# 64-bit weights to float32 with one joining in place of two, and new due times, in an attention and two-layer kernel

## The chip, the cores and the metric

The kernel runs on one core of a Trainium2 chip. The metric is the device time of one execution in microseconds (us); lower is better. The engines are called TensorE (PE in the rows, its weight loads PEld), VectorE (DVE), ScalarE (ACT), GpSimd (POOL) and SyncE (SP, which issues nearly all DMAs).

## What is computed

Random-feature attention over 4 batches, 8 heads, 576 tokens, head size 64 and 128 features, then two dense layers on the 2304 x 512 result, each with 2048 hidden units. The attention inputs and the result are float32, the dense weights come as float64.

```python
def phi(x):
    proj = np.einsum('bhsd,md->bhsm', x, omega)
    h = proj - np.sum(x * x, axis=-1, keepdims=True) / 2.0
    return np.exp(h - np.max(h, axis=-1, keepdims=True)) / np.sqrt(m)
num = phi(q) @ (phi(k).T @ v);  den = phi(q) @ phi(k).sum(tokens) + 1e-06
x = num / den                              # 2304 x 512
x = softplus(x @ w_in) @ w_out             # layer 0
out = silu(x @ w_in2) @ w_out2             # layer 1
```

The weights reach the chip as pairs of words: each float64 value is an int64 element whose low word comes first.

## The kernel before, in words

Products in the dense layers are made exact with split operands: a float32 operand is cut into a rounded part (ScalarE, a cast to fp32r) and the rest (VectorE or GpSimd, a subtraction; the helper `diff`, L296), and three matmuls take the place of one. From the middle of layer 0 on, products go by a seven-product scheme for 2 x 2 blocks, which needs sums and differences of weight blocks and of activations.

The work has these stages on TensorE:

- Start-up: the features of the first batch (`k_half`, `k_tail`, `q_half`: projection `pp`, exponentials `phi`, products `pkv`, transposes `pq`, `pn`, and back-transposes `px`). Inputs and weights are being loaded meanwhile.
- `first_layer`: three blocks of 512 tokens, each with 16 hidden chunks of 12 matmuls (tile `h`, L903 to L905), between which the next batches' attention is done. Its hidden tiles are copied out of PSUM by ScalarE (`g`, L909) and stored.
- `last_block`, `second_product(0)`, `first_product`, `second_product(1)`: the seven-product stages, lines L1192, L1032 and L1038. In `second_product`, VectorE forms combinations `t` of hidden tiles (L965) and the low halves of `g` (L296), which TensorE's products consume.

The weights are turned into float32 by `unpack`. The high word, read as a float32, holds sign, exponent and 20 bits of the mantissa, so scaling it by 2^-112 (ScalarE, `scale`, L378) gives the value shifted right by three bits. Then VectorE shifts the low word right by 29 (`shift`, L382), joins the scaled word shifted left by three with these three bits (`low_bits`, L387), and joins the sign of the high word (`sign`, L392). `weights` calls it for the 16 chunks of layer 0's input weights (tile `wf`); `sums_of` calls it 48 times for the other three weight matrices (tile `sums`), forms the block sums (L454) and stores them (`ws`), from where they are loaded as `w`. `unpack` gets a due time (`due`) from `sums_of` and none from `weights`.

All instructions are first put down as items with engine, cost, predecessors, tiles and due time (`Order.add`). `Order.run` then writes one fixed order for each engine: it always takes the item that could start first, and among those about equal the one due first. The constants at the head of the file steer it. `STAY` favours on TensorE an item that keeps the array's tiling mode. `EARLY` says how many of the first inputs lie in the ring `wa` (seven places); the others lie in `wb` (six places). `FOLD` says for which parts of the first batch (k, the tail of k, q) the squared norm is added by extra matmuls into the projection (L612) and not by a reduce and two small operations on VectorE (L580, L635, L636). `HALVES` says how many chunks of each block of `first_layer` are done as two halves of 256 tokens. `BEGIN`, `SHARE`, `LATE`, `PREP` and others are due times. In the engines' queues the order is strict: an instruction that waits holds all behind it.

Of the kernel before, what the change touches and what calls it, by code (L numbers as in the profile page):

```python
# [9 lines left out]
F32R = mybir.dt.float32r  # L10
I64 = mybir.dt.int64
U32 = mybir.dt.uint32
AF = mybir.ActivationFunctionType
ALU = mybir.AluOpType
AX = mybir.AxisListType
# [31 lines left out]


G1, G2, G3, G4 = 0.2267, 0.117, 0.224, 0.112
STAY = 7.06  # L50
GT, TURN = 0.09, 0.1
V5, V2, VS = (0.60, 0.15), (0.33, 0.15), (0.265, 0.15)
VF, VA, VH = (0.33, 0.15), (0.20, 0.15), (0.35, 0.15)
A5, A2, AE, AL = (0.52, 0.37), (0.30, 0.37), (1.0, 0.37), (0.97, 0.37)
TABLE = 1.28
G5 = (1.05, 0.4)
POOLED = False
POOL_LOW = 5
PIPE = 0.25
FROM = {"PE": 4.9, "ACT": 4.1, "DVE": 4.1, "SP": 0.8, "POOL": 2.0}  # L60
SLACK = 0.08
EARLY = 3
PLACE = {"kv": "y", "flip": "y", "num": "bank", "back": "bank"}
FIRST = {"k": "by", "q": "yy", "kv": "b", "flip": "b", "num": "y", "back": "y"}
FOLD = (True, True, False)
HALVES = (0, 0, 0)
LEAD, TRAIL, EVERY, WINDOW_OF, FETCH = 0.15, 2.58, 3.25, 81.05, 33.77
DIRECT = True
BACKLOG, SOON = 0.05, 11.94
EARLIER = (141.14, 35.66)  # L70
AHEAD, WAIT = 3.67, 4.07
RATE = 360e3
PER_BYTE, PER_ROW = 2.44e-6, 6.35e-4
ARRIVE = 2.3
MARGIN, FIRM = 0.8, 48.79
ISSUE = 0.5
BEGIN = 27.42
SHARE = (1.54, 2.37, 1.27)
AHEAD_OF = 2
FIRST_B = 2  # L80
LATE = (1.6, -2.7, 5.1, 11.0, 24.0, 18.8, 36.8, 37.3)
PREP = (100.9, 121.9, 150.8, 139.3, 176.3, 192.2, 198.9, 230.4, 231.0, 236.3, 249.1, 310.7, 369.4, 342.5, 337.7, 341.8, 563.8, 553.3, 588.5, 599.5, 593.6, 615.0, 609.1, 621.7, 103.9, 120.2, 133.9, 145.7, 170.4, 185.3, 195.1, 229.9)


def mm(n):
# [12 lines left out]
class Order:  # L98
# [5 lines left out]
    def add(self, eng, cost, fn, deps=(), due=None, alloc=(), uses=(), table=None, nbytes=0, after=0.0, loose=False, behind=None, wait=0.0, tiled=False, turn=None, row=2048):  # L104
        occ, lag = cost if isinstance(cost, tuple) else (cost, PIPE)
        i = len(self.items)
        nbytes *= RATE * (PER_BYTE + PER_ROW / row)
        it = dict(
            i=i, eng=eng, occ=occ, lag=lag, fn=fn, deps=[d for d in deps if d is not None], due=due,
            alloc=list(alloc), table=table, nbytes=nbytes, after=after, loose=loose, behind=behind, wait=wait, tiled=tiled, turn=turn, start=None, end=None,  # L110
        )
        for t in list(alloc) + list(uses):
            t["users"].append(i)
        self.items.append(it)
        return i
# [27 lines left out]
    def run(self):  # L143
# [70 lines left out]
        while len(order) < len(items):  # L214
            best = None
            for e in free:
# [14 lines left out]
                for est, i in cand:  # L231
                    if est <= s + (SLACK if e == "PE" and items[i]["tiled"] == tiled else 0.05):
# [3 lines left out]
                        if e == "PE" and items[i]["tiled"] == tiled:  # L236
                            due -= STAY
                        if pick is None or (due, i) < pick[:2]:
# [7 lines left out]
            if it["table"] not in (None, table):  # L246
                occ += TABLE
                table = it["table"]
# [29 lines left out]
def attention_moe_moe_kernel(  # L278
# [13 lines left out]
    nc = tc.nc  # L292
# [52 lines left out]
    add, new = od.add, od.tile  # L345


    t = BEGIN
# [12 lines left out]
    def unpack(layer, fc, io, raw_tag, into, tf, first, after, due=None):  # L361

        s = {}
        name = f"{layer}_{fc}_{io}"
        traw = new(raw_tag)

        def views():
            u = s["raw"].bitcast(U32).rearrange("p (n t) -> p n t", t=2)
            return u[:, :, 0], u[:, :, 1]

        def load():
            s["raw"] = get(raw_tag, [P, DM], I64, f"raw_{name}")
            nc.sync.dma_start(s["raw"], (w1, w2)[layer][fc, :, io, :])

        def scale():
            first()
            hif = s["raw"].bitcast(F32).rearrange("p (n t) -> p n t", t=2)[:, :, 1]
            nc.scalar.activation(into(), hif, AF.Copy, scale=2.0**-112)  # L378

        def shift():  # L380
            lo, _ = views()
            nc.vector.tensor_scalar(lo, lo, 29, None, op0=ALU.logical_shift_right)  # L382

        def low_bits():
            lo, _ = views()
            fu = into().bitcast(U32)
            nc.vector.scalar_tensor_tensor(fu, fu, 3, lo, op0=ALU.logical_shift_left, op1=ALU.bitwise_or)  # L387

        def sign():
            _, hi = views()  # L390
            fu = into().bitcast(U32)
            nc.vector.scalar_tensor_tensor(fu, hi, 0x80000000, fu, op0=ALU.bitwise_and, op1=ALU.bitwise_or)  # L392

        opens = not tf["users"]
        a = add("SP", (ISSUE, 0), load, alloc=[traw], nbytes=P * DM * 8, row=4096, after=after, due=due)
        b = add("ACT", (0.575, 0.37), scale, [a], alloc=[tf] if opens else [], uses=[traw] + ([] if opens else [tf]))
        c = add("DVE", VF, shift, [a], uses=[traw])
        d = add("DVE", V5, low_bits, [b, c], uses=[traw, tf])
        return add("DVE", V5, sign, [d], uses=[traw, tf]), b, (s, traw)

    def weights(fc, after):
        s = {}
# [23 lines left out]
        f = add("ACT", A5, high, [r], alloc=[tw] if opens else [], uses=[tf] + ([] if opens else [tw]))  # L426
        wready[fc] = add(*(("POOL", G5) if fc < POOL_LOW else ("DVE", V5)), low, [f], uses=[tf, tw])
        wkept[fc] = add("SP", (ISSUE, 0), lambda: nc.sync.dma_start(wf[pair][:, e], s["f"]), [r], uses=[tf], nbytes=P * DM * 4, row=DM * 4)
# [96 lines left out]
    def inputs(s, name, xT, xN, vs, fold, held, after):  # L525

        lane = "wa" if len(early) < EARLY else "wb"
        early.append(name)
# [44 lines left out]
        def square():  # L573
            if fold and not here:
                s["nat"] = get("ld", [P, 512], F32, f"xq_{name}")
            nc.scalar.activation(s["nat"], s["xt"] if fold else s["nat"], AF.Square)

# [8 lines left out]
        if held and POOLED:  # L586
            sq = add("POOL", G5, lambda: nc.gpsimd.tensor_tensor(s["nat"], s["nat"], s["nat"], op=ALU.mult), [ln], uses=[tn])
        else:
# [4 lines left out]
    def features(s, name, simple, fold, ins, cols, sq_of, psums):  # L593
# [24 lines left out]
        for j in range(2):  # L618
# [21 lines left out]
            if simple or direct:  # L640
# [3 lines left out]
                def exp(j=j, opens=opens):  # L644
# [6 lines left out]
                    for q in range(4):  # L651
                        nc.scalar.activation(phi[:, q], s["pp"][j][:, q], AF.Exp, bias=s["nb", j][:, q : q + 1])  # L652
                    s["phi", j] = phi
# [11 lines left out]
        if not (simple or direct):  # L665

            def exp():
                both = s["both"]
                nc.scalar.activation(both, both, AF.Exp)
                s["phi", 0], s["phi", 1] = both[:, 0], both[:, 1]  # L670
# [260 lines left out]
    def second_product(layer, t0):  # L931
# [6 lines left out]
        def unit(q, sc, t0, tws, wload, wt):  # L938
# [6 lines left out]
            def load_b(i, j):  # L945
# [11 lines left out]
                if layer == 0:  # L957
                    got[i, j] = add("ACT", on_act(n), lambda s=s: nc.scalar.activation(s["b", i, j], s["b", i, j], AF.Softplus), [got[i, j]], uses=[tb[i, j]], table="softplus")

# [210 lines left out]
    def units(layer, sc, xop, xo, weight, t0):  # L1170

        def unit(k):
# [36 lines left out]
            def gated(key, i, j, dep, due, x=None, s=s, bank=bank, hold=hold, un=un, k=k, sc=sc):  # L1209
                if x is None:  # L1210
                    th = s["th", key]
                    a = dep if layer == 0 else add("ACT", on_act(HW_), lambda: nc.scalar.activation(s[key], s[key], AF.Silu), [dep], uses=[th], due=due, table="silu")  # L1212
                else:
# [254 lines left out]
    t = last_block(chain_at)  # L1468
    t = second_product(0, t)
    t = first_product(t)  # L1470
# [66 lines left out]
```

## Time and profile before

| | |
|---|---|
| median of 3 runs | 852.03 us |
| lowest, highest | 851.89, 853.98 us |
| the profiled execution | 852.56 us |
| its span, first to last instruction | 850.8 us |
| TensorE busy | 840.7 us (99%) |
| VectorE busy | 708.6 us (83%) |
| ScalarE busy | 550.7 us (65%) |
| granted TensorE clock | 1.0 throughout |

Busy times are shares of the span of one profiled execution. TensorE's matmuls are pipelined, so its busy time can hide short stalls. A wait is named by the engine and line that released it.

### The profile page before, as it was taken

What the parts mean: (1) busy time and instruction counts of PE and PEld (TensorE: products, weight loads), DVE (VectorE), ACT (ScalarE), POOL (GpSimd) and SP (SyncE); (2) the same over time, 40 slices, a digit from 0 to 9 for tenths busy, and PEclk for the clock granted to TensorE, in tenths of its full rate; (3) what the DMA queues carried; (4) which work ended last, traced back from release to release, by engine and by line L of the source; (5) the groups of instructions that cost most, each with busy time, mean ns of one, the idle gap of its engine ahead of it and who ended that gap; (6) DMA issues with size and microseconds to landing.
All of it is one profiled execution on the core that took longest, in us unless ns stands there. A gap on an engine that the chain in (4) does not pass through costs nothing.

```text
span 850.8 us, 17355 instructions
## 1 busy us (share of the span) xinstructions
PE 840.7 (99%) x6436; PEld 798.1 (94%) x6436; DVE 708.6 (83%) x1275; ACT 550.7 (65%) x1056; POOL 7.8 (1%) x13
## 2 busy tenths in 40 slices
PE   9899999999999999999999999999999999999998
PEld 7787888888889999999999999999999999999998
DVE  5999978878789699999999995764766897899973
ACT  8968757557667579768665685755766744654330
POOL 0110000000000000000000000000000000000000
PEclk9999999999999999999999999999999999999999
DMA  9879889988869999899987696677688865497432
GB/s 331 280 250 352 304 259 350 318 274 277 289 237 321 327 347 341 278 304 306 305 289 235 220 310 214 212 256 254 217 297 308 336 223 178 156 323 240 164 118 75
DMA packets 128756, 227.06 MB, mean 267 GB/s; under 512 B 11680, under 2 KB 87584, under 8 KB 128672
## 3 DMA queue, kind: packets, MB, share of 16 engines
q1 hardware_dynamic: 128528, 225.83, 78.1%
q8 instruction: 50, 0.82, 0.4%
q14 instruction: 34, 0.28, 0.1%
q10 hardware_dynamic: 144, 0.13, 0.1%
HBM read 138.89 MB, written 87.03 MB: 266 GB/s over the span
## 4 chain that ended last, share of the span: by engine, by line
PE 77%; DVE 9%; DMA 6%; ACT 4%; issue 2%; SPq 0%; POOL 0%; DVEq 0%; ACTq 0%; POOLq 0%
PE X L1192 14%; PE X L1038 12%; PE Z L1192 7%; PE Z L1038 6%; PE h L903 6%; PE h L905 5%; PE h L904 5%; PE Y L1192 4%; PE X L1032 3%; DVE g L296 3%; PE Y L1038 3%; DMA w<-ws 2%; PE pn_q L302 2%; PE pp_q L608 2%; PE pkv_k L302 2%
## 5 line engine op out<-in xcount | busy, mean ns | idle before, releaser
L1038 PE MATMUL X<-w,g 128*128 128x256 f32 x864 | 106.8, 283 | 0.0
L1192 PE MATMUL X<-x_x,w 128*128 128x384 f32 x576 | 105.8, 334 | 0.0
L1038 PEld LDWEIGHTS X<-w,g 128*128 128x128 f32 x864 | 105.1, 192 | 0.0
L1032 PE MATMUL X<-g,w 128*128 128x384 f32 x576 | 103.8, 335 | 1.0 <-DVE g L296 1.0
L1032 PEld LDWEIGHTS X<-g,w 128*128 128x128 f32 x576 | 100.0, 188 | 2.0 <-DVE g L296 2.0
L980 ACT CAST g<-b 128x768 fp32r<-128x768 f32 x96 | 77.9, 836 | 35.9 <-PE X L1038 16.1
L1192 PEld LDWEIGHTS X<-x_x,w 128*128 128x128 f32 x576 | 100.4, 188 | 0.0
L980 ACT CAST g<-t 128x768 fp32r<-128x768 f32 x72 | 58.3, 835 | 63.2 <-DVE t L965 39.2
L296 DVE TENSOR_TENSOR g<-b,g 128x768 fp32r<-128x768 f32 x96 | 89.3, 950 | 7.3 <-ACT g L980 7.2
L903 PE MATMUL h<-x,wt 128*128 128x512 f32 x192 | 78.5, 409 | 1.3 <-ACT g L909 1.3
L296 DVE TENSOR_TENSOR g<-t,g 128x768 fp32r<-128x768 f32 x72 | 67.4, 950 | 10.8 <-ACT g L980 10.6
L905 PE MATMUL h<-x,wt 128*128 128x512 f32 x192 | 75.1, 391 | 0.0
L904 PE MATMUL h<-x,wt 128*128 128x512 f32 x192 | 75.0, 390 | 0.0
L1038 PE MATMUL Z<-w,g 128*128 128x256 f32 x432 | 53.8, 283 | 0.0
L1192 PE MATMUL Z<-x_x,w 128*128 128x384 f32 x288 | 53.8, 334 | 0.0
L1212 ACT ACTIVATE s<-s 128x384 f32<-128x384 f32 x72 | 37.4, 525 | 25.2 <-DVE s L1207 24.8
L1038 PEld LDWEIGHTS Z<-w,g 128*128 128x128 f32 x432 | 52.7, 192 | 0.0
L1032 PE MATMUL Z<-g,w 128*128 128x384 f32 x288 | 51.9, 334 | 0.0
L652 ACT ACTIVATE phi_q<-pp_q,mn_q 128x128 f32<-128x128 f32 x144 | 41.6, 485 | 15.2 <-DVE mn_q L636 9.3
L296 DVE TENSOR_TENSOR w<-w 128x1024 fp32r<-128x1024 f32 x42 | 50.6, 1214 | 0.6 <-ACT w L477 0.5
L1192 PEld LDWEIGHTS Z<-x_x,w 128*128 128x128 f32 x288 | 50.3, 188 | 0.0
L1032 PEld LDWEIGHTS Z<-g,w 128*128 128x128 f32 x288 | 50.1, 188 | 0.0
(144 smaller groups left out, 1592.9 us busy)
## 6 DMA issues: line engine op xcount, KB each, us to landing
b<-gate SPq DMA_DIRECT2D x48, 768.0 KB, 6.7
raw<-in_w SPq DMA_DIRECT2D x64, 512.0 KB, 5.7
gate<-s SPq DMA_DIRECT2D x128, 192.0 KB, 3.0
w<-ws SPq DMA_DIRECT2D x42, 512.0 KB, 5.4
gate<-g SPq DMA_DIRECT2D x48, 256.0 KB, 3.6
ws<-sums SPq DMA_DIRECT2D x48, 256.0 KB, 3.4
ws<-raw SPq DMA_DIRECT2D x24, 384.0 KB, 3.8
x_q<-in_qT SPq DMA_DIRECT2D x18, 256.0 KB, 5.1
```

The source lines that it names most:

```text
L296: nc.vector.tensor_tensor(o, a, b, op=ALU.subtract)
L302: nc.tensor.matmul(o[r], a[:, r], b, **flags)
L608: nc.tensor.matmul(pp[j][:, q], s["xt"][r, c : c + P], om_sb[r, :], start=True, stop=not fold)
L652: nc.scalar.activation(phi[:, q], s["pp"][j][:, q], AF.Exp, bias=s["nb", j][:, q : q + 1])
L903: nc.tensor.matmul(ph, wt[:, 0, cs], xt[:, 0, ts], start=(opens and cc == 0), stop=False, skip_group_check=part is not None)
L904: nc.tensor.matmul(ph, wt[:, 0, cs], xt[:, 1, ts], start=False, stop=False, skip_group_check=part is not None)
L905: nc.tensor.matmul(ph, wt[:, 1, cs], xt[:, 0, ts], start=False, stop=(cc == NCC - 1), skip_group_check=part is not None)
L980: nc.scalar.copy(g[:, :, 0], s[src][:, 2 * r : 2 * r + 2])
L1032: nc.tensor.matmul(o[:, :HW_], w[:, a, 2 * r + k, cs], g[:, k, h], start=one, stop=(k == 1 and a == 1), skip_group_check=True)
L1038: nc.tensor.matmul(o[:, a * 256 : a * 256 + 256], g[:, k, h, ts], w[:, v, 2 * r + k], start=one, stop=(k == 1 and h == 1), skip_group_chec ...
L1192: nc.tensor.matmul(s[x][:, :HW_], w[:, a, cs], xop[p][:, cc, h], start=(opens and cc == 0 and a == 0 and h == 0), stop=(cc == 1 and a == 1 ...
L1212: a = dep if layer == 0 else add("ACT", on_act(HW_), lambda: nc.scalar.activation(s[key], s[key], AF.Silu), [dep], uses=[th], due=due, tab ...
```

## The change

In `unpack`, the two joinings become one. There are two forms, chosen by whether a due time was given (`LOW3`). For the 16 weights of `weights`, VectorE copies the sign bit by a byte operation from the top byte of the high word into the top byte of the shifted low word, and one joining takes both. For the 48 tiles of `sums_of`, ScalarE copies the top byte of the low word into the bottom byte of the high word, VectorE shifts the high word right by five and masks it so that sign and the three low bits remain, and one joining takes both. Besides, constants are new: `STAY`, `EARLY` from 3 to 1, `FOLD` for the tail of k from folded to not folded, `HALVES` from none to two chunks of the first block, and the due times.

```diff
-STAY = 7.06
+STAY = 4.34
+LOW3 = (False, True)
-EARLY = 3
+EARLY = 1
-FIRST = {"k": "by", "q": "yy", "kv": "b", "flip": "b", "num": "y", "back": "y"}
-FOLD = (True, True, False)
-HALVES = (0, 0, 0)
-LEAD, TRAIL, EVERY, WINDOW_OF, FETCH = 0.15, 2.58, 3.25, 81.05, 33.77
+FIRST = {"k": "yb", "q": "yy", "kv": "b", "flip": "b", "num": "y", "back": "y"}
+FOLD = (True, False, False)
+HALVES = (2, 0, 0)
+LEAD, TRAIL, EVERY, WINDOW_OF, FETCH = 0.05, 2.57, 3.0, 135.89, 32.22
-BACKLOG, SOON = 0.05, 11.94
-EARLIER = (141.14, 35.66)
-AHEAD, WAIT = 3.67, 4.07
+BACKLOG, SOON = 0.05, 9.76
+EARLIER = (159.99, 25.05)
+AHEAD, WAIT = 3.72, 4.72
-MARGIN, FIRM = 0.8, 48.79
+MARGIN, FIRM = 0.87, 17.28
-BEGIN = 27.42
-SHARE = (1.54, 2.37, 1.27)
+BEGIN = 28.74
+SHARE = (1.57, 2.42, 1.16)
-FIRST_B = 2
+FIRST_B = 1
...
+        def byte(i):
+            return s["raw"].bitcast(U8).rearrange("p (n t) -> p n t", t=8)[:, :, i]
...
+        def low_byte():
+            nc.scalar.copy(byte(4), byte(3))
+
+        def signed():
+            hi = s["raw"].bitcast(I32).rearrange("p (n t) -> p n t", t=2)[:, :, 1]
+            nc.vector.tensor_scalar(hi, hi, 5, -0x7FFFFFF9, op0=ALU.arith_shift_right, op1=ALU.bitwise_and)
+
         def shift():
             lo, _ = views()
             nc.vector.tensor_scalar(lo, lo, 29, None, op0=ALU.logical_shift_right)
 
-        def low_bits():
-            lo, _ = views()
+        def sign():
+            nc.vector.tensor_scalar(byte(3), byte(7), 0x80, None, op0=ALU.bitwise_and)
+
+        def join(i):
             fu = into().bitcast(U32)
-            nc.vector.scalar_tensor_tensor(fu, fu, 3, lo, op0=ALU.logical_shift_left, op1=ALU.bitwise_or)
-
-        def sign():
-            _, hi = views()
-            fu = into().bitcast(U32)
-            nc.vector.scalar_tensor_tensor(fu, hi, 0x80000000, fu, op0=ALU.bitwise_and, op1=ALU.bitwise_or)
+            nc.vector.scalar_tensor_tensor(fu, fu, 3, views()[i], op0=ALU.logical_shift_left, op1=ALU.bitwise_or)
...
         b = add("ACT", (0.575, 0.37), scale, [a], alloc=[tf] if opens else [], uses=[traw] + ([] if opens else [tf]))
-        c = add("DVE", VF, shift, [a], uses=[traw])
-        d = add("DVE", V5, low_bits, [b, c], uses=[traw, tf])
-        return add("DVE", V5, sign, [d], uses=[traw, tf]), b, (s, traw)
+        if LOW3[due is not None]:
+            c = add("ACT", (0.575, 0.37), low_byte, [b], uses=[traw])
+            d = add("DVE", VF, signed, [c], uses=[traw])
+            i = 1
+        else:
+            c = add("DVE", VF, shift, [a], uses=[traw])
+            d = add("DVE", VF, sign, [c], uses=[traw])
+            i = 0
+        return add("DVE", V5, lambda: join(i), [b, d], uses=[traw, tf]), b, (s, traw)
```

The lists `LATE` and `PREP` (the due times of the 8 late sums and of the 32 groups of sums) are new as well, each entry moved by up to 16 us; the order in which the groups come stays much the same.

## Rows read from the trace of the kernel before

**Rows 1.** Waits of TensorE, whole span: line, releaser: us in total, times, longest.

```profile
PE pn_q L302 <- ACT phi_q L652: 1.3, 2, 1.0
PE h L903 <- ACT g L909: 1.3, 1, 1.3
PE X L1032 <- DVE g L296: 1.0, 3, 0.5
PE px_q L820 <- DVE den_q L809: 0.8, 1, 0.8
PE pn_q L302 <- ACT qt_q L790: 0.7, 2, 0.4
```

**Rows 2.** Timeline of TensorE, 408 to 442 us: start, us, work, [idle before, releaser].

```profile
411.00 4.28 PE L1032 MATMUL X<-g,w 128*128 128x384 f32 x23 [0.31 <-DVE g L296]
...
428.40 8.41 PE L1032 MATMUL X<-g,w 128*128 128x384 f32 x47 [0.47 <-DVE g L296]
...
441.41 0.79 PE L1032 MATMUL X<-g,w 128*128 128x384 f32 x3 [0.25 <-DVE g L296]
```

**Rows 3.** Busy time in three stretches: us, then PE, PEld, DVE, ACT, POOL.

```profile
15.00:45.00 30.00, 26.69 (x433) 23.14 (x431) 28.48 (x86) 29.12 (x85) 2.57 (x2) 1.00 0.87 303
45.00:75.00 30.00, 28.73 (x272) 23.66 (x272) 29.66 (x68) 23.31 (x64) 3.88 (x3) 1.00 0.83 282
325.00:500.00 175.00, 173.97 (x1001) 172.97 (x1000) 174.04 (x235) 124.36 (x162) 0.00 (x0) 1.00 0.85 282
```

**Rows 4.** Timeline of TensorE at 70 us, columns as in rows 2.

```profile
70.61 0.50 PE L903 MATMUL h<-x,wt 128*128 128x512 f32 x1 [1.27 <-ACT g L909]
```

**Rows 5.** Timeline of ScalarE ahead of that wait.

```profile
61.64 2.18 ACT L652 ACTIVATE phi_k<-pp_k,mn_k 128x128 f32<-128x128 f32 x8 [3.11 <-DVE mn_k L635]
...
69.86 0.69 ACT L909 COPY g<-h 128x512 f32<-128x512 f32 x1
```

**Rows 6.** Timeline of VectorE, 64 to 66 us.

```profile
64.41 0.68 DVE L392 SCALAR_TENSOR_TENSOR wf<-raw,wf 128x512 uint32<-128x512 uint32 x1
65.02 0.68 DVE L387 SCALAR_TENSOR_TENSOR wf<-wf,raw 128x512 uint32<-128x512 uint32 x1
65.62 0.42 DVE L382 TENSOR_SCALAR raw<-raw 128x512 uint32<-128x512 uint32 x1
65.95 0.68 DVE L392 SCALAR_TENSOR_TENSOR wf<-raw,wf 128x512 uint32<-128x512 uint32 x1
```

**Rows 7.** VectorE by line, 300 to 441 us: count, busy us, mean ns, idle before.

```profile
L387 DVE SCALAR_TENSOR_TENSOR sums<-sums,raw 128x512 uint32<-128x512 uint32 x10 | 6.7, 686 | 0.3 <-ACT sums L378 0.3
```

**Rows 8.** The same view of VectorE, 45 to 61.64 us.

```profile
L392 DVE SCALAR_TENSOR_TENSOR wf<-raw,wf 128x512 uint32<-128x512 uint32 x4 | 4.2, 1038 | 0.0
```

**Rows 9.** Timeline of all engines at 56 us.

```profile
56.06 1.28 POOL L421 TENSOR_TENSOR wt<-wf,wt 128x512 fp32r<-128x512 f32 x1 [3.42 <-ACT wt L417]
...
56.44 1.44 DVE L392 SCALAR_TENSOR_TENSOR wf<-raw,wf 128x512 uint32<-128x512 uint32 x1
```

**Rows 10.** Timeline of VectorE in the start-up.

```profile
17.26 0.15 DVE L635 SCALAR_TENSOR_TENSOR mn_q<-sqs_q,mn_q 128x4 f32<-128x4 f32 x1
```

**Rows 11.** The chain that ended last, in order of time: start, us, work.

```profile
445.69 4.16 PE Y L1032 x24
...
834.63 4.32 PE X L1038 x36
```

**Rows 12.** Timeline of TensorE at 38.9 us.

```profile
38.91 0.41 PE L820 MATMUL px_q<-ident,xn_q 128*128 128x128 f32 x2 [0.77 <-DVE den_q L809]
```

**Rows 13.** Timeline of SyncE's queue, the last early loads of q.

```profile
9.92 1.23 SPq L546 DMA_DIRECT2D x_q<-in_qN  x2
```

**Rows 14.** Timeline of TensorE, 17 to 25 us.

```profile
17.61 2.09 PE L302 MATMUL pkv_k<-x_k,phi_k 128*64 128x65 f32 x64
...
24.61 2.59 PE L608 MATMUL pp_q<-om_sb,x_q 64*128 64x128 f32 x32
```

**Rows 15.** DMA issues of the page: count, KB each, median us to landing.

```profile
x_q<-in_qN SPq DMA_DIRECT2D x18, 256.0 KB, 5.6
```

More of the change, by code (lines that the diff above doesn't have):

```diff
@@ L12 @@
 U32 = mybir.dt.uint32
+I32 = mybir.dt.int32
+U8 = mybir.dt.uint8
 AF = mybir.ActivationFunctionType
@@ L74 @@
 ARRIVE = 2.3
-MARGIN, FIRM = 0.8, 48.79
+MARGIN, FIRM = 0.87, 17.28
 ISSUE = 0.5
-BEGIN = 27.42
-SHARE = (1.54, 2.37, 1.27)
+BEGIN = 28.74
+SHARE = (1.57, 2.42, 1.16)
 AHEAD_OF = 2
-FIRST_B = 2
-LATE = (1.6, -2.7, 5.1, 11.0, 24.0, 18.8, 36.8, 37.3)
-PREP = (100.9, 121.9, 150.8, 139.3, 176.3, 192.2, 198.9, 230.4, 231.0, 236.3, 249.1, 310.7, 369.4, 342.5, 337.7, 341.8, 563.8, 553.3, 588.5, 599.5, 593.6, 615.0, 609.1, 621.7, 103.9, 120.2, 133.9, 145.7, 170.4, 185.3, 195.1, 229.9)
+FIRST_B = 1
+LATE = (0.4, 1.9, 10.0, 7.3, 33.1, 20.2, 38.6, 40.8)
+PREP = (100.7, 121.3, 148.2, 125.9, 176.3, 188.3, 196.7, 225.9, 226.5, 232.6, 242.2, 304.8, 383.4, 352.8, 348.9, 353.3, 547.6, 550.0, 594.8, 602.8, 596.9, 626.0, 621.9, 637.2, 102.2, 124.9, 145.0, 139.9, 173.2, 196.6, 191.1, 220.6)
 def mm(n):
```

## The prediction

> **What bounds the kernel now.** I read the list of TensorE's waits first, because TensorE is busy for 99% of the span and every microsecond saved has to come out of its idle time or its work. After its first memset it waited for five things worth naming, 5.1 us in all [rows 1]: 2.8 us in the start-up (on the exponentials, on the copies of transposed features and on the denominators), 1.3 us for ScalarE to copy a hidden tile out of PSUM, and 1.0 us for VectorE's `g` halves. So the change can only move the end by a few microseconds, however much VectorE work it takes away. The timeline of TensorE places them: the VectorE ones are three waits at 411, 428 and 441 us [rows 2], the ScalarE one is at 70.6 us [rows 4]. From 442 us to the end none is listed.
>
> Then I read the busy time of each engine in the stretches that lead to these waits [rows 3]. From 15 to 45 us VectorE is busy 28.48 of 30 us and ScalarE 29.12: both are full. From 45 to 75 us VectorE is full (29.66 of 30) and ScalarE is not (23.31). From 325 to 500 us VectorE is full (174.04 of 175) while ScalarE has 50 us free. So VectorE is the late engine behind the waits at 411 to 441 us, and also behind the one at 70.6 us: there ScalarE stood idle for 3.11 us until 61.64 us on VectorE's row maxima, and made the copy that TensorE was waiting for at 69.86 us [rows 4, 5].
>
> **The change, part by part.** *The joining that goes.* On VectorE a 64-bit weight tile costs a shift and two joinings, each of 512 elements. In VectorE's timeline a joining starts 0.60 to 0.61 us before the next instruction and a shift 0.33 us before it [rows 6]; these distances, not the durations, are what an instruction occupies.
>
> A tile of the 48 for the sums loses one joining on VectorE (0.60) and its shift becomes a shift-and-mask of the same shape. That form is not in the trace: its nearest row is the shift at 0.33 [rows 6], the other end is a joining, 0.60; I take 0.33, as both have one source and the same strided words. A gain is excluded, because it reads and writes as many elements as the shift. So a tile saves 0.60 (bound 0.33).
>
> In exchange ScalarE copies 512 bytes. The nearest row is ScalarE's copy of 512 elements, 0.69 us long [rows 5]; the bounds are zero and 0.69 for each. From 300 to 441 us ten such tiles pass [rows 7]. At most 10 x 0.69 = 6.9 us go onto ScalarE, which has 50 us free in the overlapping stretch [rows 3], so I cost this at nothing. If that cover were gone, the softplus and `g` casts queued behind would be late.
>
> VectorE gains 10 x 0.60 = 6.0 us (bound 3.3) before the last of three waits that are 0.31 + 0.47 + 0.25 = 1.03 us together [rows 2]. Either bound covers them: **-1.03 us**. What is late next there is TensorE itself. The three waits make up the whole of what this stretch can give back.
>
> *The 16 first-layer weights.* Here the shift stays and the sign joining becomes a byte operation on VectorE, also not in the trace. Its ends are the shift (0.33) and the joining (0.60) [rows 6]; I take the shift again, because it has one source in SBUF as well, so a tile saves 0.27, with 0 as the bound. ScalarE's work is unchanged. Between 45 and 61.64 us four sign joinings pass [rows 8], all ahead of the row maxima that ScalarE then waited for: 4 x 0.27 = 1.08 us earlier, against a wait of 1.27 us at 70.6 us [rows 4]. I take **-1.08 us** (bounds 0 and -1.27). Of these four, two met a GpSimd subtraction: the one at 56.44 us took 1.44 us while GpSimd worked from 56.06 us for 1.28 us, and the four average 1038 ns against 686 elsewhere [rows 7 to 9].
>
> The Trainium skill (Advanced Engine Details and Errata, VectorE Performance Modes) says that VectorE's second port is shared with GpSimd and that two-port VectorE instructions and GpSimd ones block each other; the collision in the trace fits that. By this rule the byte operation, if it runs at the shift's rate, is held up in the same way and each of the two held tiles still saves 0.27; if it ran on one port, it would take about a joining's time but escape, and the sum would differ by less than the bound of 0 to -1.27 already set.
>
> *The tail of k, no longer folded* (`FOLD[1]`). TensorE loses 16 small matmuls, which I value at nothing since TensorE goes on to wait in the start-up [rows 1]. VectorE gains a reduce of 512 elements (taken at a joining's 0.60, which is one element at a time too) and four small operations of 0.15 [rows 6, 10]: 0.60 + 4 x 0.15 = 1.20 us on an engine that is full. SyncE gains one load of 256 KB. Before the first hidden tile two weights are needed (chunks 0 and 1), which give back 2 x 0.27 = 0.54. So +0.66 us (bounds 0, if other order hides it, and +1.20).
>
> *Two chunks in halves* (`HALVES`). 24 matmuls of 512 columns become 48 of 256. A group of 24 at 384 columns takes 4.16 us and one of 36 at 256 columns 4.32 [rows 11]: 0.1733 and 0.1200 each, so 0.053 for 128 columns and 0.013 for the instruction itself. 24 more cost 24 x 0.013 = +0.32 us. The first halves need only the first 256 tokens, so they can run in the wait at 38.9 us (0.77 [rows 12]): -0.77. Together -0.45 us (bounds +0.32 and -2.5, the latter if the earlier start-up waits were filled too).
>
> *The rest of the constants* (`STAY`, `EARLY`, the due times) reorders all queues. No row prices a new order; I take 0 with 1 us either way, besides the cases below.
>
> The sum against the profiled execution: -1.03 - 1.08 + 0.66 - 0.45 = -1.90; 852.56 - 1.90 = 850.66 us. That execution lies 0.53 above the median of the three runs (852.03), so the forecast for a median is **850.1 us**.
>
> **The rivals.** *More of the start-up closes* (faster still). The new order with early halves fills the waits of the start-up and the h wait: -1.03 - 1.27 - 2.8 + 0.32 = -4.78, so 847.3 us. For it: TensorE's waits there are short and several, and the halves are new work to put in. Against it: ScalarE is busy 29.12 of 30 us there [rows 3], and the change takes nothing from it.
>
> *A wait takes the place of the joining* (no change). Before, the shift waited for a load alone; now VectorE's first step on a sums tile waits for two ScalarE steps. VectorE's queue is in order, so the `g` halves stand behind it, and TensorE's products behind those. If each of the ten tiles holds VectorE up by the byte copy's 0.69 [rows 5], 6.9 us are lost and the 6.0 are eaten; it decides from 0.5 us a tile on, where less than 1 us is left. The sum is then without the 1.03: -0.87, 851.2 us. Against it: in that stretch VectorE idled only 0.3 us on ScalarE for the whole of the joinings' group, which waits for ScalarE's scaling already [rows 7].
>
> *The change does not do what it says.* If operations on bytes and on the shift-and-mask run at a joining's rate, weights save nothing: -1.03 (the sums still lose one instruction, 0.33) + 1.20 - 0.45 = -0.28, 851.8 us; if they are slower than any row, the 1.03 goes too, 852.8 us.
>
> *The start-up slips* (slower). With `EARLY` 1, one of the first nine inputs lies in the ring `wa` and eight in `wb`, which has six places. The eighth must wait for the third k input, whose last reader on TensorE is in the run that starts at 17.61 and lasts 2.09 us. Before, the last q inputs were issued by 9.92 + 1.23 = 11.15 us; now at 19.7 us, landing 5.6 us later at 25.3, where their projection ran at 24.61 us [rows 13 to 15]: 0.7 us late. With the k tail's 1.20 unhidden and the halves' 0.32 unfilled the start-up slips by 2.2 us, and ScalarE, being full, can't make it up. Less the 1.03 this is +1.2: 853.2 us. It decides from a slip of 1.03 us on, and if the weights save nothing besides.
>
> **How the numbers follow.** Forecast 850.1 us: 0.46 (its own range, by the bounds of its terms, 848.6 to 851.8). Start-up closes, 847.3: 0.24. A wait takes the joining's place, 851.2: 0.13. The operations are slow, 851.8 to 852.8: 0.07. The start-up slips, 853.2: 0.10. The range takes in all but the far half of the second case and the far half of the last: 847.4 to 853.4 us.
>
> A measurement of this kernel tells 0.3% (2.6 us) from no change, so faster means below 849.5 and slower above 854.6. Faster: the second case less a little (0.22) and the lower third of the forecast's range (0.16), 0.38. Slower: the far end of the slip, 0.06. Same: 0.56.
>
> **What would show each step.** In the changed profile: the joining has 64 instructions and not 128; VectorE's busy time falls by some 30 us and ScalarE's rises by 25 to 33; VectorE is no longer full from 325 to 500 us and TensorE's waits on `g` are gone; the wait of TensorE on ScalarE's copy of `h` is short or gone; the start-up waits add up to 2 to 3 us, and the first product of a hidden tile starts no later than before. It is wrong if VectorE idles on ScalarE before the shift-and-mask, if the byte operations take over 0.7 us, or if TensorE's waits before 45 us grow past 5 us.

## The result, and the profile after

The changed kernel takes 857.39 us (median of 6 runs, 856.43 to 860.08) against 851.96 us of the kernel before (6 runs): a ratio of 1.0065, 95% interval 1.0048 to 1.0082. It is slower by some 5.4 us, where 850.1 was forecast and 853.4 was the upper end. The profiled execution took 858.36 us with a span of 856.6; that of before had a span of 850.8.

The page of the changed kernel says that the work did move as described:

```profile
PE 843.7 (99%) x6444; PEld 799.7 (93%) x6444; DVE 682.7 (80%) x1232; ACT 602.1 (70%) x1104; POOL 8.2 (1%) x13
```

VectorE's busy time fell from 708.6 to 682.7 us, but ScalarE's rose from 550.7 to 602.1, by 51 us where at most 33 had been allowed. The groups of instructions of the new unpacking (line, engine, operation, tiles; count; busy us, mean ns of one; idle time before them and what ended it) say why:

```profile
L387 ACT COPY raw<-raw 128x512 uint8<-128x512 uint8 x48 | 66.5, 1404 | 0.3
L384 ACT ACTIVATE sums<-raw 128x512 f32<-128x512 f32 x48 | 32.9, 689 | 6.4 <-issue 3.1 <-DMA raw<-in_w 3.0
L391 DVE TENSOR_SCALAR raw<-raw 128x512 int32<-128x512 int32 x48 | 20.5, 428 | 58.2 <-ACT raw L387 54.5 <-DMA wl<-wl 1.7 <-DMA ws<-raw 1.6
L398 DVE TENSOR_SCALAR raw<-raw 128x512 uint8<-128x512 uint8 x16 | 11.8, 754 | 0.0
```

The shift-and-mask answers [rows 6] as forecast: 428 ns, like a shift. The other two new forms do not: the byte copy on ScalarE takes 1404 ns, twice the 689 ns of the scaling of as many words in the row below it, and the byte AND on VectorE 754 ns, more than a joining (686 ns in [rows 7]). And VectorE stood idle for 54.5 us before the shift-and-mask, waiting for the byte copy. Most of that idle time costs nothing (VectorE has 20% to spare), some does.

Where TensorE fell behind is read from its timeline, at the first matmul of each long stage (start, us, work). Changed kernel:

```profile
260.93 2.27 PE L1208 MATMUL X<-xl,wt 128*128 128x384 f32 x12
...
496.45 2.24 PE L1208 MATMUL X<-x_x,w 128*128 128x384 f32 x12
848.28 4.48 PE L1054 MATMUL X<-w,g 128*128 128x256 f32 x36
```

and before:

```profile
256.37 2.27 PE L1192 MATMUL X<-xl,wt 128*128 128x384 f32 x12
491.29 2.24 PE L1192 MATMUL X<-x_x,w 128*128 128x384 f32 x12
843.11 4.48 PE L1038 MATMUL X<-w,g 128*128 128x256 f32 x36
```

TensorE is 4.56 us late when the products of `last_block` begin (260.93 against 256.37), 5.16 us late at 496 us and 5.17 at its last group. So nearly all of the loss arises before 261 us, and what follows up to 496 us, with the stretch that I had looked at most (300 to 441 us), adds 0.6. The remaining 0.6 of the span (5.8 in all) is the tail behind the last matmul.

The waits of TensorE in the changed kernel (releaser: us in total, times, longest), against [rows 1]:

```profile
PE pn_q L305 <- ACT phi_q L668: 2.3, 3, 1.4
PE X L1048 <- DVE g L299: 1.7, 2, 1.4
PE px_q L836 <- DVE xn_q L828: 1.0, 2, 0.8
PE pq_q L802 <- ACT phi_q L668: 0.9, 2, 0.7
PE px_q L836 <- DVE den_q L825: 0.6, 1, 0.6
PE pp_k L624 <- DVE x L299: 0.3, 1, 0.3
```

The wait on the copy of `h` [rows 4] is gone; the waits on exponentials (`phi_q`) have grown, and so have those on the denominators and what is multiplied by them (`den_q`, `xn_q`: 1.6 us instead of 0.8); the `g` waits are 1.7 us instead of 1.0. Two places in the timelines show what stands ahead of the late engines. VectorE, in the stage of the first-layer weights:

```profile
73.60 0.97 DVE L395 TENSOR_SCALAR raw<-raw 128x512 uint32<-128x512 uint32 x2
74.48 1.34 DVE L398 TENSOR_SCALAR raw<-raw 128x512 uint8<-128x512 uint8 x2
75.60 1.33 DVE L402 SCALAR_TENSOR_TENSOR wf<-wf,raw 128x512 uint32<-128x512 uint32 x2
76.83 0.17 DVE L825 TENSOR_SCALAR den_q<-pn_q 128x4 f32<-128x4 f32 x1
```

The denominators, four small steps that TensorE's next transposes need, stand behind 3.2 us of unpacking. Between these starts a byte AND occupies 0.56 us (1.12 for two) and a joining 0.62. Then ScalarE (first two lines) and VectorE (last two), where the first sums are prepared:

```profile
107.36 2.57 ACT L387 COPY raw<-raw 128x512 uint8<-128x512 uint8 x2
109.60 0.75 ACT L925 COPY g<-h 128x512 f32<-128x512 f32 x1
...
108.75 0.43 DVE L391 TENSOR_SCALAR raw<-raw 128x512 int32<-128x512 int32 x1 [1.76 <-ACT raw L387]
...
111.03 0.69 DVE L299 TENSOR_TENSOR x<-px_q,x 128x512 fp32r<-128x512 f32 x1
```

A byte copy occupies ScalarE for 1.12 us (109.60 less 107.36, for two). VectorE's queue waits 1.76 us for the first of them, in front of the step on `x` at 111.03, for which TensorE waits next (0.33 us at 111.78, `pp_k` in the list above). That is the order of events of the rival "a wait takes the place of the joining", at 108 us already and not only in the stretch from 300 us where I had put it.

### The profile page after: what moved, and what is told of

Read it like the earlier page. It is cut to its first block, busy times and chain, and to the rows that moved or that the text cites. A ratio compares the mean times of both kernels' runs of the same rounds, so it can differ in the third digit from the quotient of the medians.

```text
span 856.6 us, 17401 instructions
## 1 busy us (share of the span) xinstructions
PE 843.7 (99%) x6444; PEld 799.7 (93%) x6444; DVE 682.7 (80%) x1232; ACT 602.1 (70%) x1104; POOL 8.2 (1%) x13
## 4 chain that ended last, share of the span: by engine, by line
PE 65%; DVE 12%; DMA 7%; ACT 5%; issue 3%; SPq 1%; DVEq 0%; ACTq 0%
PE X L1208 14%; PE X L1054 12%; PE Z L1208 7%; PE Z L1054 6%; PE Y L1208 4%; DMA raw<-in_w 4%; PE X L1048 3%; DVE g L299 3%; PE Y L1054 3%; PE h L919 3%; PE h L921 3%; PE h L920 3%; DVE t L981 2%; PE Z L1048 1%; ACT raw L387 1%
## 5 line engine op out<-in xcount | busy, mean ns | idle before, releaser
L919 PE MATMUL h<-x,wt 128*128 128x512 f32 (+1 forms) x200 | 80.0, 400 | 0.0
L921 PE MATMUL h<-x,wt 128*128 128x512 f32 (+1 forms) x200 | 76.5, 383 | 0.0
L920 PE MATMUL h<-x,wt 128*128 128x512 f32 (+1 forms) x200 | 76.3, 382 | 0.0
L391 DVE TENSOR_SCALAR raw<-raw 128x512 int32<-128x512 int32 x48 | 20.5, 428 | 58.2 <-ACT raw L387 54.5
L387 ACT COPY raw<-raw 128x512 uint8<-128x512 uint8 x48 | 66.5, 1404 | 0.3
```

What stands on the lines that cost most here:

```text
L387: nc.scalar.copy(byte(4), byte(3))
L391: nc.vector.tensor_scalar(hi, hi, 5, -0x7FFFFFF9, op0=ALU.arith_shift_right, op1=ALU.bitwise_and)
L919: nc.tensor.matmul(ph, wt[:, 0, cs], xt[:, 0, ts], start=(opens and cc == 0), stop=False, skip_group_check=part is not None)
L920: nc.tensor.matmul(ph, wt[:, 0, cs], xt[:, 1, ts], start=False, stop=False, skip_group_check=part is not None)
L921: nc.tensor.matmul(ph, wt[:, 1, cs], xt[:, 0, ts], start=False, stop=(cc == NCC - 1), skip_group_check=part is not None)
```

## The experiments

My theory after the result, called "bytes" below: the byte steps are twice as long as the rows that I took for them, and that alone makes the loss. The rival, "order": the new due times and constants lose the time whatever the unpacking costs.

**One step made word-wide.** The changed kernel, the same order of all queues, with ScalarE's byte copy replaced by a copy of the high words onto themselves:

```
-            nc.scalar.copy(byte(4), byte(3))
+            w = s["raw"].bitcast(F32).rearrange("p (n t) -> p n t", t=2)[:, :, 1]
+            nc.scalar.copy(w, w)
```

> The changed kernel with its order of instructions untouched; only ScalarE's byte copy on a sums tile becomes an in-place copy of the high word as float32 (512 elements, the same stride), so the three lowest bits of these weights come from the wrong byte. Theory bytes (the copy takes 1.4 us where the planner's order allows 0.575, and VectorE's queue waits behind it): the copy takes 0.6 to 0.7 us, VectorE's idle time before its shift-and-mask falls from 58 us to under 15, and the time falls from 857.4 to 851 to 853 us. Theory constants (the newly searched order is itself worse): the time stays at 856 to 858 us whatever the copy takes.

It took 854.58 us (852.95 to 855.82), ratio to before 1.0025 [1.0014, 1.0036]. The byte copy in place of a word copy costs 2.8 us. My expectation of 851 to 853 us was missed, and so was its mark of under 15 us for VectorE's wait before the shift-and-mask: it fell from 58.2 us to 38.6 us only. In its trace the 48 copies fall to two thirds of a microsecond, and the place where TensorE was late closes in part:

```profile
L388 ACT COPY raw<-raw 128x512 f32<-128x512 f32 x48 | 31.7, 667 | 0.3
...
258.47 2.27 PE L1209 MATMUL X<-xl,wt 128*128 128x384 f32 x12
492.65 2.24 PE L1209 MATMUL X<-x_x,w 128*128 128x384 f32 x12
```

TensorE reaches the last block at 258.47 us in place of 260.93, and the second stage at 492.65 in place of 496.45: 2.46 us of the gain arise before the last block and another 1.34 behind its start, where the waits on `g` fall from 1.7 us to 0.3. So against the word copy the stretch from 300 us costs something too. From 62 to 160 us VectorE's wait for the copy of the first six tiles falls from the first of these rows (changed kernel) to the second:

```profile
L391 DVE TENSOR_SCALAR raw<-raw 128x512 int32<-128x512 int32 x6 | 2.6, 432 | 9.5 <-ACT raw L387 9.4
...
L392 DVE TENSOR_SCALAR raw<-raw 128x512 int32<-128x512 int32 x6 | 2.6, 428 | 5.1 <-ACT raw L388 4.5 <-DMA gate<-g 0.6
```

**Both steps made word-wide.** The same, and the byte AND of the first-layer weights replaced by an AND on words:

```
-            nc.vector.tensor_scalar(byte(3), byte(7), 0x80, None, op0=ALU.bitwise_and)
+            nc.vector.tensor_scalar(views()[0], views()[0], 7, None, op0=ALU.bitwise_and)
```

> As word_copy (same order of instructions as the changed kernel), and VectorE's byte AND on the 16 first-layer weights becomes an AND on words of 512 elements, so the sign of these weights is left out. Theory partial writes (all writes of less than a word at a pitch of 8 bytes cost too much, on both engines): the AND takes 0.43 us for 0.75, the 2.0 us that TensorE lost at 74 to 78 us shrink to under 1, and the time falls from 854.6 to 852 to 853.3 us. Theory order (what word_copy has left above the kernel before comes from the new order of the start-up): the time stays at 854 to 855 us.

852.34 us (11 runs, 851.47 to 852.98), ratio 1.0000 [0.9992, 1.0009]. The byte AND costs another 2.2 us, and the two together 5.0 of the 5.4: the loss is explained by the two byte steps, and the expected 852 to 853.3 us came. But the forecast gain of 1.9 us is not there either, with exactly the durations that I had assumed. I come back to that below.

**What it is about the bytes.** The changed kernel with eleven forms of a step on 128 x 512 elements behind it, three of each, on nothing's path:

```
+    for _ in range(3):
+        nc.scalar.copy(p8[:, :, 4], p8[:, :, 3])
+    for _ in range(3):
+        nc.scalar.copy(pf, p8[:, :, 3])
...
```

> The changed kernel with rows of single operations of 512 elements appended after all work, on a scratch tile, to price element size and stride by themselves. If writing less than a word is what costs on ScalarE, byte and half-word writes take 1.4 us both and a byte read into float32 0.6 to 0.7; if the byte type costs, half-words take 0.6 to 0.7 and bytes without a stride 1.4 too; if the stride costs, the float32 copy from and to every second word takes 1.4 as well and unstrided bytes 0.6. On VectorE the same for the byte AND (0.75 us in the changed kernel) against half-words and words (0.42). The time of the whole is the changed kernel's plus 30 to 40 us.

Four of the forms on ScalarE (groups by line), then four on VectorE (timeline; three of each):

```profile
L1509 ACT COPY probe_raw<-probe_raw 128x512 uint16<-128x512 uint16 x3 | 4.1, 1377 | 0.1
L1515 ACT COPY probe_raw<-probe_raw 128x512 uint8<-128x512 uint8 x3 | 2.3, 760 | 0.1
L1511 ACT COPY probe_raw<-probe_raw 128x512 f32<-128x512 f32 x3 | 1.9, 641 | 0.1
L1513 ACT COPY probe_raw<-probe_raw 128x512 uint8<-128x512 uint8 x3 | 1.9, 617 | 0.1
...
858.19 2.28 DVE L1517 TENSOR_SCALAR probe_raw<-probe_raw 128x512 uint8<-128x512 uint8 x3 [6.12 <-ACT probe_raw L1515]
860.50 2.27 DVE L1519 TENSOR_SCALAR probe_raw<-probe_raw 128x512 uint16<-128x512 uint16 x3
862.81 1.35 DVE L1521 TENSOR_SCALAR probe_raw<-probe_raw 128x512 uint32<-128x512 uint32 x3
864.20 1.35 DVE L1523 TENSOR_SCALAR probe_raw<-probe_raw 128x512 uint8<-128x512 uint8 x3
```

L1509 writes two bytes of every eight, L1511 a word of every eight bytes, L1515 a byte of every four, L1513 bytes side by side; L1517, L1519 and L1521 write one, two and four bytes of every eight, L1523 bytes side by side. The three other forms, one line each:

```profile
L1503 ACT COPY probe_raw<-probe_raw x3: 1377/1377/1381, 837.3 to 840.1; 128x512 uint8<-128x512 uint8 x3
L1505 ACT CAST probe_f<-probe_raw x3: 655/655/710, 841.2 to 842.7; 128x512 f32<-128x512 uint8 x3
L1507 ACT CAST probe_raw<-probe_f x3: 1362/1363/1364, 843.4 to 846.2; 128x512 uint8<-128x512 f32 x3
```

L1503 is the byte copy itself. L1505 only reads bytes at the pitch of eight and writes words side by side: 655 ns, no slower than a copy of words. L1507 only writes bytes at that pitch: 1363 ns. So on ScalarE it isn't the type and not the reading; it is writing less than a word at a pitch of eight bytes. VectorE's forms show the same step, 736 and 734 ns against 428; reading and writing were not tried apart there. The run took 868.26 us, 10.9 more than the changed kernel and not the 30 to 40 that I had expected: ScalarE's rows lie beside the last products, from 837 us on.

**The new unpacking alone.** The unpacking of the change with every constant and due time of before:

```
-STAY = 4.34
+STAY = 7.06
...
-PREP = (100.7, 121.3, 148.2, 125.9, 176.3, ...
+PREP = (100.9, 121.9, 150.8, 139.3, 176.3, ...
```

> The new unpacking under all the constants of the kernel before. Theory bytes: slower than before by 3 us or more (855 to 860 us), with VectorE idle on ScalarE's byte copy for tens of microseconds. Theory constants: 851 to 852.5 us, as before.

858.76 us (857.16 to 861.77), ratio 1.0078 [1.0063, 1.0092]: the unpacking alone loses as much as the whole change, as "bytes" had expected. The same kernel with both steps word-wide, as above:

> The new unpacking under the constants of the kernel before, with both byte operations replaced by word operations (the three lowest bits wrong, the first-layer signs left out), against unpack_only with 858.8 us. Theory partial writes: the byte operations are what made unpack_only slow; 850.5 to 852.5 us. Theory order: any new unpacking under due times that were searched for another one loses some microseconds; 855 us or more.

855.09 us, ratio 1.0035 [1.0021, 1.0048]. The byte writes cost 3.7 us in this order too. But 2.8 us stay: due times that were searched for the old unpacking do not suit the new one even at its ideal price. "Bytes" had expected 850.5 to 852.5, so it missed here.

**The new constants alone.** The old unpacking (shift and two joinings) with the constants and due times of the change:

```
-            c = add("ACT", (0.575, 0.37), low_byte, [b], uses=[traw])
-            d = add("DVE", VF, signed, [c], uses=[traw])
...
+        d = add("DVE", V5, low_bits, [b, c], uses=[traw, tf])
+        return add("DVE", V5, sign, [d], uses=[traw, tf]), b, (s, traw)
```

> All new constants with the old unpacking (shift and two joinings on VectorE, nothing on ScalarE beside the scaling). Theory bytes: 850 to 852.5 us, not slower than before. Theory constants: 856 us or more.

864.47 us, ratio 1.0142 [1.0127, 1.0157]. The number of "order" (856 or more) came; mine missed by 12 us. Its list of TensorE's waits has one on a `last_block` tile and six on `g`:

```profile
PE X L1193 <- DVE s L1208: 3.9, 1, 3.9
PE X L1033 <- DVE g L297: 2.9, 6, 1.0
```

The new due times hand VectorE the second joining's work where there is no longer room for it. Still "order" does not name the cause: the new order loses this with an unpacking for which it was not made, and with the new unpacking at word price it equals before. TensorE has no wait at all between 60 and 80 us here; I come back to that.

**The planner told the true prices.** In the changed kernel the planner's costs of the two byte steps are set to about what they occupy:

```
-            c = add("ACT", (0.575, 0.37), low_byte, [b], uses=[traw])
+            c = add("ACT", (1.1, 0.37), low_byte, [b], uses=[traw])
...
-            d = add("DVE", VF, sign, [c], uses=[traw])
+            d = add("DVE", (0.67, 0.15), sign, [c], uses=[traw])
```

> The changed kernel, complete, with the planner told what the two byte operations occupy (1.1 us on ScalarE for 0.575, 0.67 on VectorE for 0.33), so it writes an order that knows them. Theory partial writes: the planner can hide a part, 853 to 856 us. Theory order: a rewritten order is as bad or worse than the one searched, 857 to 862 us.

860.33 us, ratio 1.0096 [1.0081, 1.0112], 2.9 us slower than the change itself, and within what "order" had expected. Right costs with due times that were searched with other costs are no improvement; the due times would have to be searched again.

**The tail of k folded again.** The kernel with both steps word-wide, and one constant put back:

```
-FOLD = (True, False, False)
+FOLD = (True, True, False)
```

> As word_both, but the tail of k is folded again as in the kernel before (TensorE gets 16 small matmuls back, VectorE loses a reduce and four small operations in the start-up). If the unfolded tail is what delays the start-up, the first units start 0.6 to 1.2 us earlier than in word_both; if the start-up is late for other reasons, they start within 0.5 us of it, or later.

857.43 us, ratio 1.0059 [1.0045, 1.0072]: 5.1 us slower than without this edit. TensorE's longest wait on `phi_q` becomes 2.4 us (1.4 before the edit), and the first product of a hidden tile starts at 45.91 us and not at 43.06: later, as expected if the start-up is late for other reasons than the unfolded tail. This doesn't price the unfolded tail; it shows that one constant put back moves the order by more than all the terms of my sum.

**The same idea without byte writes.** In the order of the changed kernel, with all bits of the weights kept. ScalarE reads the byte and writes a whole word with the three bits; VectorE joins that word and the sign with a joining:

```
-            nc.scalar.copy(byte(4), byte(3))
+            lo = s["raw"].bitcast(I32).rearrange("p (n t) -> p n t", t=2)[:, :, 0]
+            nc.scalar.activation(lo, byte(3), AF.Copy, bias=-15.5 / 32, scale=1.0 / 32)
...
-            nc.vector.tensor_scalar(hi, hi, 5, -0x7FFFFFF9, op0=ALU.arith_shift_right, op1=ALU.bitwise_and)
+            nc.vector.scalar_tensor_tensor(hi, hi, 0x80000000, lo, op0=ALU.bitwise_and, op1=ALU.bitwise_or)
...
-            nc.vector.tensor_scalar(byte(3), byte(7), 0x80, None, op0=ALU.bitwise_and)
+            nc.vector.scalar_tensor_tensor(lo, hi, 0x80000000, lo, op0=ALU.bitwise_and, op1=ALU.bitwise_or)
```

> The order and the costs of the changed kernel, but no byte is written at a pitch of eight. ScalarE reads the lowest 32 bits' top byte and writes a whole word with the three bits (the probe's 655 ns for that form, against 1404 of the byte copy); VectorE joins that word and the sign with a joining (0.60 occupied, where the changed kernel has 0.33 for the shift-and-mask of a sum and 0.67 for the byte AND of a first-layer weight). All bits of the weights are kept, as in the changed kernel. Theory 'bytes' (the width of the byte writes is what costs): as the kernel with word-wide steps in both places, 852.3, plus what 48 joinings in place of 48 shifts cost where VectorE is full; from its start-up and first stage (some 20 of these tiles, 0.27 each, about a third of them beside a full VectorE) 1 to 3 us, so 853 to 855.5, and clearly below the changed kernel's 857.4. Theory 'order' (the new order loses whatever the unpacking): 856.5 or more.

856.75 us, ratio 1.0053 [1.0036, 1.0070], within reach of the changed kernel, above what "bytes" had expected and at the number of "order" (856.5 or more). The groups and TensorE's timeline show both halves of it:

```profile
L388 ACT ACTIVATE raw<-raw 128x512 int32<-128x512 uint8 x48 | 32.4, 682 | 0.0
L392 DVE SCALAR_TENSOR_TENSOR raw<-raw 128x512 uint32<-128x512 uint32 x48 | 33.1, 691 | 41.2 <-ACT raw L388 39.5 <-DMA gate<-s 1.5
...
258.73 2.27 PE L1210 MATMUL X<-xl,wt 128*128 128x384 f32 x12
...
415.37 5.77 PE L1050 MATMUL X<-g,w 128*128 128x384 f32 x23 [2.16 <-DVE g L299]
495.86 2.24 PE L1210 MATMUL X<-x_x,w 128*128 128x384 f32 x12
```

Up to the last block the loss of the byte copy is gone (258.73, beside 258.47 with the word copy and 260.93 with bytes). That of the byte AND is not (256.72 and 257.13 with both steps word-wide, below): a joining, which takes its place, occupies 0.60 us where the AND occupied 0.56. Then 48 joinings where the change has 48 steps of 428 ns bring a wait of 2.16 us on `g`, where VectorE is full in every one of these kernels. Behind this wait the granted clock falls (0.72 of full speed from 415 to 421 us), and the 23 products in the fourth line take 5.77 us where 23 took 4.28 before [rows 2]: 1.5 us more. At 495.86 TensorE is as late as in the changed kernel (496.45). My expectation had put these joinings' price into the first stage, 1 to 3 us, and 1.6 to 2.0 us of it fell due there; the wait and the clock it had not.

**Before and the word-wide kernel once more**, for second traces:

> The kernel with word-wide steps in both places once more (the first-layer weights lose their signs), for a second trace. In its first trace TensorE's last matmul ended 1.2 us earlier than in the kernel before and the stores after it took 1.0 us longer. If the longer tail is chance, the last matmul ends at 846 to 847 again and the tail is 3.2 to 3.6; if it belongs to the order, the tail is 4 or more again.

> The kernel before once more, for a second trace. Last matmul at 847.6 and tail 3.2 as in its first trace, if these are steady; if the tail varies by 1 us from execution to execution, it can be 4 here.

They took 852.69 and 851.97 us in one run each. The first product of the last block, in the word-wide kernel, in its repetition and in the repetition of before:

```profile
256.72 2.27 PE L1209 MATMUL X<-xl,wt 128*128 128x384 f32 x12
...
257.13 2.27 PE L1209 MATMUL X<-xl,wt 128*128 128x384 f32 x12
...
256.93 2.27 PE L1192 MATMUL X<-xl,wt 128*128 128x384 f32 x12
```

The last group of matmuls, in the same three:

```profile
841.91 4.48 PE L1055 MATMUL X<-w,g 128*128 128x256 f32 x36
...
842.72 4.48 PE L1055 MATMUL X<-w,g 128*128 128x256 f32 x36
...
842.52 4.48 PE L1038 MATMUL X<-w,g 128*128 128x256 f32 x36
```

It starts at 841.91 and 842.72 us with the word-wide kernel, at 843.11 (above) and 842.52 with the kernel before: the means are 0.5 us apart, less than two executions of one kernel. The spans end 8.7 and 8.2 us after that start in the word-wide kernel (850.6 and 850.9) and 7.7 us after it in both traces of before (850.8 and 850.2). So the tail is 0.5 to 1.0 us longer there, and eats what is left; the repetition, whose last products end at 847.2 us with a tail of 3.7, lies between the two cases of its expectation. The last two stores of 64 KB took 2.5 and 2.9 us (medians) to land, and 2.0 in both traces of before; why, I have not settled.

The waits on `g` in the repeated kernel before are what I had not looked for:

```profile
440.83 4.26 PE L1032 MATMUL X<-g,w 128*128 128x384 f32 x23 [0.22 <-DVE g L296]
```

One wait of 0.22 us stands where the first trace has three of 1.03 us [rows 2].

## Why the prediction was wrong

**The step that failed** is the price of the byte operations. I took ScalarE's byte copy at "zero and 0.69 for each", from a copy of 512 elements [rows 5], and the byte AND between "the shift (0.33) and the joining (0.60)" [rows 6]. The copy occupies ScalarE for 1.12 us and its result comes after 1.40: outside the bounds, because every one of my rows writes whole words. The byte AND occupies 0.56, inside its bounds but at the far end, and its result comes after 0.75. The experiments give the two together 5.0 us (2.8 and 2.2), where the sum had the copy at nothing and the AND as a gain.

**The joining that goes (-1.03).** Whether the mechanism holds at the price that I assumed is not shown: with word-wide steps the three waits are gone in one trace and 0.34 us in the other, but before they are 1.03 us in one execution and 0.22 in the next, so 0.2 to 1.0 was to be had, not 1.03. In the changed kernel they are 1.72 us instead. My sign that VectorE is no longer full from 325 to 500 us did not come either: of 175 us it is busy 171.85 in the changed kernel and 174.38 with both steps word-wide, 174.04 before [rows 3]. And "I cost this at nothing" looked only at the stretch from 300 to 441 us, where ScalarE has room. The first six tiles pass between 106 and 160 us, where VectorE's queue holds `first_layer`'s steps behind the join; there the cover was not free.

**The 16 first-layer weights (-1.08).** The wait at 70.6 us [rows 4] is gone, but not for the reason that I gave: it is gone with the new constants and both joinings too, and under the old constants 0.76 us of it stays with the new unpacking and none with the AND on words. So the reason fits with the old order and the price that I assumed; that the wait went in the changed kernel is luck. A weight there saves 0.60 - 0.56 = 0.04 us, so 0.16 for the four and not 1.08, and the later weights stand ahead of the denominators (74 to 77 us above). The AND on words in its place is worth the 2.2 us between the two first experiments.

**Tail of k and halves (+0.66 and -0.45).** The forecast had TensorE fill its start-up waits. The busy time by stretch (us, then PE, PEld, DVE, ACT, POOL, granted clock) shows the opposite, in the changed kernel:

```profile
28.00:32.00 4.00, 1.65 (x34) 1.30 (x34) 3.79 (x15) 4.00 (x18) 0.00 (x0) 1.00 1.08 362
32.00:36.00 4.00, 3.63 (x40) 2.86 (x40) 3.48 (x11) 4.00 (x13) 0.00 (x0) 0.67 0.98 344
```

and before:

```profile
28.00:32.00 4.00, 2.66 (x45) 2.23 (x43) 3.60 (x14) 4.00 (x18) 0.00 (x0) 1.00 0.96 310
```

TensorE is busy 1.65 us of these 4 and not 2.66, with ScalarE full in both. Yet the first product of a hidden tile, a half of 256 tokens now, starts at 43.23 us and not at 44.93 (before). What each of the two constants did is open, since one put back rewrites the whole order.

**The sum.** With ideal prices it should have been -1.9; it was 0.0 [-0.7, +0.8, from the ratio's interval]. Up to the last block TensorE is 0.2 to 0.35 us later than before (256.72 and 257.13 us, against 256.37 and 256.93), where the three terms of the first stages were to give 0.87 us together. What it gains behind that, 0.8 us on average up to its last group, the longer tail takes back. So the forecast's mechanism bought next to nothing even where its prices held; why the first stages gave nothing is open. The range of the forecast itself was added up wrongly: with all terms at their bounds it is 847.2 to 852.5 us and not 848.6 to 851.8. The measured 857.4 lies outside both.

**The rivals.** "A wait takes the place of the joining" named the right mechanism and gave 851.2: VectorE's queue held up behind ScalarE's byte step. It had only the later of the two places, and 0.69 us a tile. "The operations are slow" named the right cause, but for steps "slower than any row" it lost no more than what I had forecast as gain (852.8); nothing in the list priced a slow step where VectorE is on the path. "The start-up slips" had the right sign, and the first half of its mechanism came, the second did not: in the changed kernel the last early load of q is issued at 18.00 us (9.92 before [rows 13], 19.7 in the rival), but the last of the three projections of q starts at 25.92, where it also was before (the second half of a run of 32 that began at 24.61 [rows 14]). SyncE's queue, then TensorE:

```profile
18.00 0.55 SPq L562 DMA_DIRECT2D x_q<-in_qN  x1
...
25.92 1.16 PE L624 MATMUL pp_q<-om_sb,x_q 64*128 64x128 f32 x16
```

Of the signs of being wrong that I had named in advance two came: VectorE idles on ScalarE before the shift-and-mask, and "the byte operations take over 0.7 us". TensorE's waits before 45 us did not grow past 5 us (3.3, on the exponentials, `den_q` and `xn_q`).

The Trainium skill (Advanced Engine Details and Errata, VectorE Performance Modes) was cited for VectorE and GpSimd blocking each other. The traces agree: in the changed kernel a shift beside GpSimd's subtraction at 56.00 us took 1.53 us, where the median is 0.43. The byte AND is held up as well: 1.26 us at 57.57 us with the word copy, and 1.76 at 51.54 us with the planner told the prices, where it takes 0.75 otherwise. So it did not escape, although it occupies about as much as a joining; that branch of the prediction did not come.

## What to carry to other kernels

An operation whose form the trace does not show must not be bounded by rows that differ in the one thing that is new in it, here the width of what is written; a few instructions of the form behind the kernel price it before anything is built on it. Look for the cost of a moved step also where its result is first needed in an engine's queue, ahead of work that the critical engine waits for, and not only where the waits were that it is to remove. Due times found for one set of costs are worth microseconds with these costs only (2.8, 12 and 5 us were lost by keeping them and changing something else), and a wait of 1 us read from one execution can be 0.2 in the next.

## What the hardware showed that I had not expected

Writing one or two bytes of every eight takes ScalarE 1363 to 1377 ns for 512 elements and VectorE 734 to 736, where words at the same pitch take 641 and 428, bytes side by side 617 and 427, and one byte of every four (ScalarE) 760. Reading bytes at the pitch of eight costs nothing extra (655). The Trainium skill (Advanced Engine Details and Errata, SBUF Cachelines) says that stride tolerance depends on the type; the trace agrees for writes, and shows nothing of it for these reads.

In the changed order the granted clock falls in the start-up: 0.67 of full speed from 32 to 36 us, so a part of this stretch at 1.2 GHz, after 4 us in which TensorE was busy for 1.65. Before, with 2.66 us busy, it stayed at 1.00. With the word copy it stayed at 1.00 too, although TensorE was busy for only 1.60 of those 4 us, so busy time alone does not tell when it falls. With both steps word-wide it fell as well (0.50 and 0.73 from 32 to 36 us). What it cost there can be read, as TensorE's order is the same in these kernels: the first product of a hidden tile starts at 43.06, 43.23 and 43.46 us where the clock fell and at 43.37 where it did not, so nothing that shows up to there. ScalarE was full in this stretch. Where TensorE has no slack, as behind the wait of 2.16 us above, the fall cost 1.5 us.
